# Talking-heads attention and two MLPs on one core: the first score tile issued by hand, loads in order of need, and the first two weight chunks decoded in v's buffers

## The chip, the core and the metric

One NeuronCore of a Trainium2 chip runs the whole program. Its engines are TensorE (PE in the profile; PEld is its weight load), VectorE (DVE), ScalarE (ACT), GpSimd (POOL) and SyncE (SP), which issues nearly all DMAs here; 16 DMA engines do the copies. Each engine takes its instructions in program order and waits on semaphores. The metric is the device time of one execution in microseconds, lower is better.

## What is computed

Three stages in a row, float32 in and out (the products are made of split halves, so that each needs three matmuls):

```python
scores = scale * q @ k^T                       # 4 batches, 12 heads, 448 x 448, head size 64
scores = einsum('bhij,hg->bgij', scores, w_pre)   # heads are mixed before the softmax
attn = softmax(scores)
attn = einsum('bhij,hg->bgij', attn, w_post)      # and after it
x = (attn @ v) as 1792 tokens x 768
x = ((x @ w1) * (x @ w2)) @ w3 @ w_out            # first MLP, 1024 wide
out = relu(x @ w_in)**2 @ w_out2                  # second MLP, 2048 wide
```

The MLP weights arrive as 64-bit floats and are decoded on the chip, chunk by chunk: two ACT and four DVE passes over 128 x 768 words per chunk, then a scale over two chunks, then two casts each.

## The kernel before

**Attention.** The rows of a batch are cut into four score tiles of 110, 110, 110 and 118 rows (`SUP`, s = 0 to 15). A tile is made by six calls of `qk` (two heads each: the q and k halves, three pairs of matmuls), whose results are copied from PSUM into the tile S (`evict_s` on ACT). A tile is then cut into blocks of 10 rows x 12 heads (180 blocks, `BLK`, u = 0 to 179). `regroup` is a DMA on SP's queue that puts a block's rows and heads on 120 partitions (`Bt`, five buffers, so block u+5 is issued when block u is done). The steps of a block are `premix` (PE), `negmax` (DVE), `expo` (ACT), `norm` for two blocks (DVE), `split_h` and, for odd blocks, `split_l` (POOL; for even ones DVE), `postmix` (PE), `at_h` (ACT), `at_l` (DVE), and `av` (PE) for a whole tile.

**What sets the order.** In the loop over u every engine's order is written out: a table of slots (`events`, filled by `at`) says at which u the loads, `qk`, `split_q`, `split_v` and so on are issued. What is ahead of the loop is ordered by the scheduler instead: the loads, the six `qk` of tile 0, the six of tile 1 (three ahead of the loop, three in slots 0, 2 and 4), the five first regroupings and the set-up of the mixing weights (`setup_mixers`). There DVE casts all halves of k and copies two thirds of the first tile out of PSUM, and POOL makes some of the low halves.

**The end of the attention.** From u = 164 (`mlp_start`) the buffers of q and k are given to the weights (pool `w`: two `raw` buffers, three `xa`, one `zt`). Chunks 0 (w1) and 1 (w2) are loaded on ACT's queue at u = 164 and 166, and decoded from u = 167 by `early = pair_steps(0, None)`, three steps a block. When a chunk has been decoded, `read_raw` issues the next load on SP's queue, into the same `raw` buffer. The attention result goes to DRAM (`store_x`) and comes back as x high halves (ACT's queue, `X_HIGH`, u = 165, 167, 169, 174) and low halves (SP's queue, u = 176). At u = 180 to 183 `first_tile` runs the first matmuls of the MLP between the last blocks.

**The MLPs** follow with their weights decoded in the background; no line of theirs is touched.

Of the kernel before, what the change touches and what calls it, by code (L numbers as in the profile page):

```python
# [35 lines left out]
def talking_heads_attention_moe_moe2(  # L36
# [181 lines left out]
    def qk(s, p, where=None):  # L218

# [15 lines left out]
        if where is None:  # L235
            Ps[s, p] = t
        else:
            for e in range(2):
                nc.vector.tensor_copy(Stile[s][:R, 2 * p + e, :], pt[e][:R, :S])
# [4 lines left out]


# [193 lines left out]
    def split_v(b, hg, i):  # L439
        t = vraw[b, hg]  # L440
        up = Vsc[b]
        if i == 0:
            Vt[b, hg] = tuple(
                bp.tile([CP, 6, NCH, D], F16, tag=f"V{x}", name=f"V{x}", bufs=3) for x in "hl"
            )
# [142 lines left out]
    load_k(0, 0)
    load_k(0, 1)
    load_q(0, 1)  # L590
    for p in (2, 3):
# [1 line left out]
    spare = bp.tile([P, NCH, H, RMAX], F16, tag="ATl", name="ATl")
    kraw[0, 2] = (
        spare.rearrange("p c h r -> p (c h r)").bitcast(F32)[:, : 2 * S]
        .rearrange("p (a s) -> p a s", a=2)
    )
    for p in (4, 5):
        nc.sync.dma_start(kraw[0, 2][:, p % 2, :], k[0, :, p, :])
# [922 lines left out]
```

## Time and profile before

| | us |
|---|---|
| median of 3 runs | 1301.48 (1300.58 to 1302.89) |
| the profiled execution | 1300.27 |
| its span | 1298.6 |
| PE busy in it | 1264.7 (97%) |
| DVE busy | 982.5 (76%) |
| ACT busy | 696.7 (54%) |
| POOL busy | 442.7 (34%), most of it in the attention |

The profile is one execution. Its timeline lists instructions by their start; a row with "x2" merges neighbours of one kind, and the bracket says how long the engine sat idle before it and what released it. The windows view gives each engine's busy time in a stretch. PEclk there is the granted clock of TensorE as a share of 2.4 GHz; in the first 29 us it reads 1.00 while the matmuls go at half the later pace, so for that stretch the durations are read and not this column.

### The profile page before, as it was taken

Reading aid. Unit: us, or ns where it says so; the run is one execution under the profiler, and the core shown is the slowest. Engines: PE = TensorE matmul, PEld = TensorE weight load, DVE = VectorE, ACT = ScalarE, POOL = GpSimd, SP = SyncE. Lnnn points to the kernel's source line nnn. Section 1 sums busy time; section 2 is a strip of 40 time slices with the busy share of each in tenths; the row PEclk is TensorE's granted clock in tenths of the full one; section 3 lists DMA queues with packets and bytes.
Section 4 is the critical chain, followed back from the end, with each engine's and each line's share of the span. In section 5 each row is a group of like instructions: output and inputs, shape, how many; then the busy total and the mean of one; then the engine's idle time right before and its main releaser. Section 6 shows DMA issues by size and latency. Waiting matters only on the chain. (4 is left out here: it accounts for less than half of the span.)

```text
span 1298.6 us, 25896 instructions
## 1 busy us (share of the span) xinstructions
PE 1264.7 (97%) x10173; PEld 778.9 (60%) x10173; DVE 982.5 (76%) x2036; ACT 696.7 (54%) x1349; POOL 442.7 (34%) x511
## 2 busy tenths in 40 slices
PE   7999999999999899999999999999999999999998
PEld 3676766667666555555559945555555555555555
DVE  5888898788888848887749777336669788797776
ACT  3877876877886534554324354236853453534420
POOL 3899789879877701100002200000000100001000
PEclk9999999999999999999999999999999999999999
DMA  6466555645546723424414323103131322224004
GB/s 169 114 158 163 135 143 125 166 122 157 154 119 186 208 79 82 126 79 115 138 39 155 114 75 60 31 3 86 37 78 47 102 58 60 78 37 108 11 9 170
DMA packets 82174, 132.92 MB, mean 102 GB/s; under 512 B 30820, under 2 KB 67812, under 8 KB 82052
## 3 DMA queue, kind: packets, MB, share of 16 engines
q1 hardware_dynamic: 75636, 121.87, 34.8%
q0 software_dynamic: 2992, 5.42, 2.9%
q10 hardware_dynamic: 3424, 3.98, 1.1%
q8 instruction: 80, 1.31, 0.5%
q14 instruction: 42, 0.34, 0.1%
HBM read 80.78 MB, written 11.92 MB: 71 GB/s over the span
## 5 line engine op out<-in xcount | busy, mean ns | idle before, releaser
L964 PE MATMUL mm<-x,w 128*128 128x448 f16 x2196 | 416.7, 353 | 0.9 <-DVE th L999 0.9
L964 PEld LDWEIGHTS <-w 128*128 128x128 f16 x2304 | 225.0, 98 | 210.4 <-issue 1.1
L1399 PE MATMUL mm<-w,g 128*128 128x384 f16 x1344 | 219.7, 326 | 0.0
L1399 PEld LDWEIGHTS <-g 128*128 128x128 f16 x1344 | 131.5, 98 | 87.5 <-issue 0.2
L272 PE MATMUL p<-Bt,wpre_k 120*120 120x448 f32 x360 | 163.3, 573 | 8.7 <-DMA Bt<-S 4.9
L338 POOL TENSOR_SCALAR EH<-E,st 120x448 f16<-120x448 f32 x180 | 134.9, 759 | 63.9 <-DVE st L324 46.4
L365 PEld LDWEIGHTS <-EH 120*112 120x112 f16 (+1 forms) x1440 | 125.3, 130 | 50.4 <-issue 40.3
L387 DVE TENSOR_TENSOR ATl<-o,ATh 112x480 f16<-112x480 f32 x180 | 116.1, 645 | 38.3 <-ACT ATh L381 38.2
L381 ACT CAST ATh<-o 112x480 f16<-112x480 f32 x180 | 100.8, 561 | 64.5 <-PE o L365 57.2
L365 PE MATMUL o<-wph,EH 120*112 120x120 f16 x720 | 124.9, 219 | 6.3 <-DVE ATl L387 4.7
L294 ACT ACTIVATE E<-p,st 120x448 f32<-120x448 f32 x180 | 115.7, 643 | 23.9 <-DVE st L286 10.7
L729 POOL DMA_DIRECT2D across<-tot x23 | 12.8, 555 | 324.1 <-ACT xa L715 324.1
L1408 DVE SCALAR_TENSOR_TENSOR acc<-mm,sv,acc 128x384 f32<-128x384 f32 x196 | 112.2, 610 | 14.2 <-PE mm L1399 13.5
L365 PE MATMUL o<-wpl,EH 120*112 120x120 f16 x720 | 122.7, 216 | 0.0
L365 PE MATMUL o<-wph,EL 120*112 120x120 f16 x720 | 122.7, 216 | 0.0
L286 DVE TENSOR_REDUCE st<-p 120x1 f32<-120x448 f32 x180 | 110.2, 612 | 9.4 <-PE p L272 9.2
L964 PE MATMUL mm<-h,M 128*128 128x448 f16 x576 | 109.8, 353 | 0.7 <-ACT M L1129 0.5
L350 POOL TENSOR_TENSOR EL<-F,EH 120x448 f16<-120x448 f32 (+1 forms) x90 | 101.6, 1129 | 7.5
L243 ACT COPY S<-s 110x896 f32<-110x896 f32 (+1 forms) x92 | 83.8, 911 | 29.2 <-PE s L232 28.5
L715 ACT ACTIVATE xa<-xa 128x768 f32<-128x768 f32 x56 | 47.1, 842 | 93.7 <-DVE xa L711 75.7
L352 DVE SCALAR_TENSOR_TENSOR EL<-E,st,EH 120x448 f16<-120x448 f32 (+1 forms) x90 | 84.1, 934 | 13.7 <-POOL EH L338 13.2
L365 PEld LDWEIGHTS <-EL 120*112 120x112 f16 x720 | 93.9, 130 | 0.0
(194 smaller groups left out, 2030.8 us busy)
## 6 DMA issues: line engine op xcount, KB each, us to landing
Bt<-S SPq DMA_DIRECT2D x176, 210.0 KB
raw<-in_moe_w_out_dram SPq DMA_DIRECT2D x24, 768.0 KB
raw<-in_moe_w_in_dram SPq DMA_DIRECT2D x16, 768.0 KB
raw<-in_moe_w_dram SPq DMA_DIRECT2D x14, 768.0 KB
raw<-in_moe_w_dram SPq DMA_DIRECT2D x16, 512.0 KB
vraw<-in_v_dram SPq DMA_DIRECT2D x24, 224.0 KB
out_dram<-acc SPq DMA_DIRECT2D x28, 192.0 KB
kraw<-in_k_dram SPq DMA_DIRECT2D x22, 224.0 KB
```

Source lines behind the costliest of these rows:

```text
L272: nc.tensor.matmul(pt[: n * H, :S], wpre_k.rearrange("p t g -> p (t g)")[: n * H, : n * H], Bt.pop(u)[: n * H], start=True, stop=True,)
L286: nc.vector.tensor_reduce(nsum[u][:n, 0, j : j + 1], Pp[u][:n, :S], axis=AX.X, op=ALU.max, negate=True)
L294: nc.scalar.activation(e[:n], Pp.pop(u)[:n, :S].rearrange("p (a b) -> p a b", a=EG), AF.Exp, bias=t[:n, 0, j : j + 1], scale=1.0, accum_ou ...
L338: nc.gpsimd.tensor_scalar(seven(EH[u][:n]), Ex[u][:n], inverse(u), 1.0, op0=ALU.mult, op1=ALU.mult)
L350: nc.gpsimd.tensor_tensor(a, f, b, op=ALU.subtract)
L352: nc.vector.scalar_tensor_tensor(a, e, inverse(u), b, op0=ALU.mult, op1=ALU.subtract)
L365: nc.tensor.matmul(pt[:CP, c * n : (c + 1) * n], a[:n, c * CP : (c + 1) * CP], w[:n, :n], start=(i == 0), stop=(i == 2),)
L381: nc.scalar.copy(ATs[s][0][:, :, :, m * NR : m * NR + nr], src)
L387: nc.vector.tensor_tensor(ATs[s][1][:, :, :, a], src, ATs[s][0][:, :, :, a], op=ALU.subtract)
L964: nc.tensor.matmul(pt[:, :S], w[a][:, cs], x[z][:, sl], start=(c == 0 and i == 0), stop=(c == len(parts) - 1 and i == 2),)
L1399: nc.tensor.matmul(pt[:, :OH], gs[j][a][:, ts_], ws[j][0][:, w, os_], start=(n == 0), stop=(n == 5),)
L1408: nc.vector.scalar_tensor_tensor(d, pt[:, :OH], sv[:, v : v + 1], d, op0=ALU.mult, op1=ALU.add)
```

## The change

- **Start.** The order ahead of the loop is written by hand. Loads go out as q, k0, k1, k2, the second half of q, k3 to k5, then tile 1's q, then the mixing weights, then the first three loads of v; v's other three are moved behind regroupings, at u = 1 to 3.
- For tile 0, ACT casts the high halves of four k pairs and copies most PSUM results, DVE makes all low halves of k, and POOL makes only low halves of q. All six `qk` of tile 1 and its copies stand ahead of block 0; in the loop the slots of tile 1 are gone.
- `keep_busy(n)` issues n matmuls of 128 x 512 zeros into a PSUM bank that nobody reads: 8 at the very start, 3 ahead of the first `premix`, and 2 at each of u = 1 to 4.
- **End.** Chunks 0 and 1 are loaded on SP's queue at u = 153 and 156 into the two buffers of `vraw`, whose last v is read by u = 154. Their decode works in a buffer of V's halves (`v_half`) and one of k's (`zt`), one or two steps a block: chunk 0 at u = 157 to 162, chunk 1 at u = 165 to 170, the scale and the casts at u = 171 to 178. The scale's small PSUM tiles are taken from another pool.
- Chunks 2 and 3 then find both `raw` buffers empty: they are loaded at u = 175, ahead of the loads of x's low halves. x's high halves are loaded at u = 167, 170, 173 and 176.

```diff
+    zeros = flat[:, 4 * S : 4 * S + 512]
+    nc.vector.memset(zeros, 0.0)
+    def keep_busy(n):
+        for _ in range(n):
+            nc.tensor.matmul(idle, zeros[:, :P], zeros, start=True, stop=True)
...
+    for hg in range(2):
+        load_q(1, hg)
     load_mixers()
+    for i in range(3):
+        load_v(0, 0, i)
...
+    setup_mask()
+    keep_busy(8)
+    split_q(0, 0, V)
+    for p in range(3):
+        split_k(0, p, V, A)
+        qk(0, p, WHERE[p])
+    split_q(0, 1, nc.gpsimd)
+    evict_s(0, 0)
...
+    for u in range(LEAD):
+        regroup(u)
+    split_q(1, 1, None)
+    split_ql(1, 1)
+    setup_premix()
     for p in range(NDC):
+        qk(1, p, WHERE[p])
...
+        if p == 2:
+            setup_mixers()
+    keep_busy(3)
+    FILL = {1: 2, 2: 2, 3: 2, 4: 2}
+    premix(0)
+    premix(1)
...
-        dma = nc.scalar if i < 2 else nc.sync
+            if i < 2:
+                t = v_raw().rearrange("p a d -> p (a d)").bitcast(I32)
+            else:
+                t = pools["w"].tile([P, 2 * DM], I32, tag="raw", name="raw", bufs=LOADS)
...
+                if i == 0:
+                    x = v_half("hl"[k]).rearrange("p h c d -> p (h c d)").bitcast(F32)
...
-    limit = [len(chunks)]
+    limit = [2]
...
-    X_HIGH = (1, 3, 5, 10)
+    X_HIGH = (3, 6, 9, 12)
+    v_last = first[NSUP - 4]
+    W_LOADS = (v_last + 18, v_last + 21)
+    c0, c1 = v_last + 22, first[NSUP - 1] - 3
...
+        if u == NB - LEAD:
+            limit[0] = len(chunks)
+            load_to(2 + LOADS)
-        if u - mlp_start in (0, 2):
-            load_to((u - mlp_start) // 2 + 1)
-        if u == mlp_start + 3:
-            early = pair_steps(0, None)
+        if u in W_LOADS:
+            load_to(W_LOADS.index(u) + 1)
+        if u == c0:
+            early = (x for x in pair_steps(0, None) if x[2])
```

DVE at the start of the program, before: casts (kh, qh), low halves (kl, ql) and copies into S alternate.

```order
L208 CAST qh<-qraw 128x330
L210 TENSOR_TENSOR ql<-qraw,qh 128x330
L183 CAST kh<-kraw 128x448
L185 TENSOR_TENSOR kl<-kraw,kh 128x448
L183 CAST kh<-kraw 128x448
L208 CAST qh<-qraw 128x330
L185 TENSOR_TENSOR kl<-kraw,kh 128x448
L183 CAST kh<-kraw 128x448 x2
L239 COPY S<-p 110x448 x2
L183 CAST kh<-ATl 128x448 x2
```

DVE at the same place, after (ATl is the spare buffer that holds k4, k5 and the zeros).

```order
L609 MEMSET ATl 128x256
L219 CAST qh<-qraw 128x330
L221 TENSOR_TENSOR ql<-qraw,qh 128x330
L193 TENSOR_TENSOR kl<-kraw,kh 128x448 x3
L219 CAST qh<-qraw 128x330
L193 TENSOR_TENSOR kl<-kraw,kh 128x448
L191 CAST kh<-ATl 128x448
L193 TENSOR_TENSOR kl<-ATl,kh 128x448
L191 CAST kh<-ATl 128x448
L193 TENSOR_TENSOR kl<-ATl,kh 128x448
```

ACT at the start, after; before, it had only copies of 110 x 896 ahead of the first exponential.

```order
L189 CAST kh<-kraw 128x448
L189 CAST kh<-kraw 128x448
L189 CAST kh<-kraw 128x448
L249 COPY S<-s 110x896
L189 CAST kh<-kraw 128x448
L255 COPY S<-p 110x448 x2
L255 COPY S<-o 110x448 x2
L249 COPY S<-s 110x896
L255 COPY S<-p 110x448
L217 CAST qh<-qraw 128x330
L255 COPY S<-o 110x448
```

Four of DVE's six casts of k and six of its eight copies of tile 0 have gone to ACT, and the two low halves of k that POOL made have gone to DVE.

SP's queue at the end of the attention, before: two loads of weights (raw) stand between the last regroupings.

```order
L266 DMA Bt<-S 120x1x448 x3
L655 DMA raw<-in_moe_w_dram 128x1536
L266 DMA Bt<-S 120x1x448
L512 DMA x_d<-xt 128x3x110 x2
L266 DMA Bt<-S 120x1x448 x2
L655 DMA raw<-in_moe_w_dram 128x1536
L266 DMA Bt<-S 120x1x448
L266 DMA Bt<-S 96x1x448
L519 DMA x<-x_d 128x6x448 x3
L519 DMA x<-x_d 128x6x220
```

SP's queue there, after, from the second early load (chunk 1 into vraw) to the loads of x.

```order
L721 DMA vraw<-in_moe_w_dram 128x1536
L529 DMA x_d<-xt 128x3x110 x2
L279 DMA Bt<-S 120x1x448 x6
L529 DMA x_d<-xt 128x3x110 x2
L279 DMA Bt<-S 120x1x448 x5
L529 DMA x_d<-xt 128x3x110 x2
L279 DMA Bt<-S 120x1x448 x4
L529 DMA x_d<-xt 128x3x110 x2
L279 DMA Bt<-S 120x1x448 x3
L279 DMA Bt<-S 96x1x448
L721 DMA raw<-in_moe_w_dram 128x1536 x2
L536 DMA x<-x_d 128x6x448 x3
```

No weight load stands between the last 18 regroupings any more; two now stand between the last of them and x.

## Rows read from the trace of the kernel before

**Rows 1.** Timeline of PE where the MLP begins: start, us, engine, line, instruction, idle before.

```profile
480.77 19.46 PE L964 MATMUL mm<-x,w 128*128 128x448 f16 x102 [0.86 <-DVE th L999]
```

**Rows 2.** Windows (stretch, length, busy per engine, clock, DMA), and POOL's waits.

```profile
30.60:60.00 29.40, 27.09 (x235) 17.74 (x235) 25.48 (x58) 25.29 (x61) 26.45 (x31) 1.00 0.50 130
60.00:100.00 40.00, 40.00 (x522) 27.89 (x520) 36.17 (x77) 31.89 (x70) 39.01 (x43) 1.00 0.55 145
...
POOL EH L338 <- DVE st L324: 16.4, 2, 14.1
```

**Rows 3.** Timeline of the start, all engines.

```profile
3.94 0.39 DVE L183 CAST kh<-kraw 128x448 fp32r<-128x448 f32 x1
...
5.54 0.39 DVE L183 CAST kh<-kraw 128x448 fp32r<-128x448 f32 x1 [0.56 <-DMA kraw<-in_k_dram]
...
11.34 0.58 PE L232 MATMUL o<-kh,ql 64*110 64x448 f32 x2
...
11.71 0.58 PE L232 MATMUL s<-kl,qh 64*110 64x448 f32 x2
...
17.14 7.23 SPq L266 DMA_DIRECT2D Bt<-S  x6
17.14 0.91 ACT L243 COPY S<-s 110x896 f32<-110x896 f32 x1 [3.53 <-PE s L232]
...
21.33 1.85 PE L272 MATMUL p<-Bt,wpre_k 120*120 120x448 f32 x2 [1.78 <-DMA Bt<-S]
...
29.55 0.62 DVE L286 TENSOR_REDUCE st<-p 120x1 f32<-120x448 f32 x1 [2.54 <-PE p L272]
...
30.63 1.25 POOL L338 TENSOR_SCALAR EH<-E,st 120x448 f16<-120x448 f32 x2 [14.09 <-DVE st L324]
...
31.24 1.76 PE L272 MATMUL p<-Bt,wpre_k 120*120 120x448 f32 x4
```

**Rows 4.** Windows of the start.

```profile
0.00:14.50 14.50, 7.88 (x31) 4.17 (x31) 8.43 (x19) 3.09 (x3) 6.21 (x13) 1.00 0.82 205
...
21.30:29.00 7.70, 7.67 (x18) 3.24 (x19) 1.25 (x2) 2.85 (x5) 0.00 (x0) 1.00 0.59 156
```

**Rows 5.** Windows of the end of the attention.

```profile
388.00:401.00 13.00, 13.00 (x170) 9.18 (x172) 11.21 (x25) 9.64 (x23) 11.92 (x16) 1.00 0.45 113
401.00:417.00 16.00, 14.73 (x204) 10.20 (x199) 13.02 (x27) 10.46 (x25) 10.75 (x13) 1.00 0.77 212
417.00:434.00 17.00, 12.48 (x133) 7.82 (x132) 14.74 (x28) 9.69 (x24) 11.91 (x12) 0.90 0.85 239
434.00:451.00 17.00, 15.33 (x324) 12.56 (x322) 15.31 (x40) 11.25 (x25) 13.61 (x14) 1.00 0.80 235
```

**Rows 6.** Timeline there: two waits of PE, SP's weight load, the clock's dip.

```profile
425.54 3.39 PE L272 MATMUL p<-Bt,wpre_k 120*120 120x448 f32 x4 [2.08 <-ACT E L294]
...
433.33 0.35 SPq L655 DMA_DIRECT2D raw<-in_moe_w_dram  x1
433.38 0.98 PE L272 MATMUL p<-Bt,wpre_k 120*120 120x448 f32 x2 [2.18 <-DMA Bt<-S]
...
426.00:429.00 3.00, 2.97 (x7) 0.97 (x6) 2.96 (x6) 1.37 (x4) 2.92 (x3) 0.50 1.01 290
```

**Rows 7.** Timeline there: a chunk's decode on DVE, and POOL beside it.

```profile
416.38 0.55 DVE L704 TENSOR_SCALAR xa<-raw 128x768 int32<-128x768 int32 x1
...
417.93 2.18 POOL L338 TENSOR_SCALAR EH<-E,st 120x448 f16<-120x448 f32 x2 [2.48 <-PE o L365]
...
419.64 1.27 DVE L711 SCALAR_TENSOR_TENSOR xa<-zt,xa 128x768 int32<-128x768 int32 x1
...
423.07 0.96 DVE L717 SCALAR_TENSOR_TENSOR xa<-raw,xa 128x768 int32<-128x768 int32 x1 [0.45 <-ACT xa L715]
```

**Rows 8.** Timeline there: the low halves of x, and the first MLP matmuls.

```profile
441.36 3.98 SPq L519 DMA_DIRECT2D x<-x_d  x4
...
451.04 3.58 PE L964 MATMUL p<-x,w 128*128 128x448 f16 x18
```

More of the change, by code (lines that the diff above doesn't have):

```diff
@@ L127, in load_mixers, with setup_mask @@
         )
-    def setup_mixers():
-        mask = bp.tile([NBK, NR], F32, name="mask", bufs=1)
+    mask = bp.tile([NBK, NR], F32, name="mask", bufs=1)
+    def setup_mask():
         nc.gpsimd.memset(ones, 1.0)
@@ L144, in setup_mixers @@
         )
+    def setup_mixers():
         wmax = bp.tile([P, 1], F32, name="wmax", bufs=1)
@@ L182, in split_k @@
         kT[b, p] = (hh, ll)
-        nc.vector.tensor_copy(hh, t)
+        if high is nc.scalar:
+            nc.scalar.copy(hh, t)
+        else:
+            nc.vector.tensor_copy(hh, t)
         if eng is not None:
@@ L198, in load_q, with split_q @@
         )
-    def split_q(s, hg, eng):
+    def split_q(s, hg, eng, high=None):
         R = SUP[s][2]
@@ L207, in split_q @@
         a = slice(3 * hg * R, 3 * (hg + 1) * R)
-        nc.vector.tensor_copy(hh[:, a], qraw[s][:, a])
+        if high is nc.scalar:
+            nc.scalar.copy(hh[:, a], qraw[s][:, a])
+        else:
+            nc.vector.tensor_copy(hh[:, a], qraw[s][:, a])
         if eng is not None:
@@ L234, in qk @@
                 )
[L235 to L239, printed above, removed]
+        Ps[s, p] = t if where is None else pt
     def evict_s(s, p):
@@ L442, in split_v @@
         if i == 0:
[L443 to L445 removed]
+            Vt[b, hg] = tuple(v_half(x)[:CP] for x in "hl")
         hf, lf = (x.rearrange("p h c d -> p (h c) d") for x in Vt[b, hg])
@@ L532, in at @@
         events.setdefault(slot, []).append((kind, len(events), f, a))
-    for s in range(1, NSUP):
+    for s in range(2, NSUP):
         b = SUP[s][0]
@@ L587, in talking_heads_attention_moe_moe2 @@
     load_q(0, 0)
[L588 to L591, printed above, removed]
+    for p in range(NDC):
         load_k(0, p)
[L593 to L599, printed above, removed]
-    load_mixers()
-    split_q(0, 0, nc.vector)
+        if p == 2:
+            load_q(0, 1)
@@ new lines, in talking_heads_attention_moe_moe2 @@
+    evict_s(0, 0)
+    for p in (1, 2):
+        if p == 1:
+            split_k(0, 3, V, A)
+        for e in range(2):
+            evict_one(0, p, e, A)
+    for p in range(3, NDC):
+        if p > 3:
+            split_k(0, p, V)
+        qk(0, p, WHERE[p])
+    evict_s(0, 3)
+    evict_one(0, 4, 0, A)
+    evict_one(0, 4, 1, V)
+    split_q(1, 0, None, A)
+    split_ql(1, 0)
+    evict_one(0, 5, 0, A)
+    evict_one(0, 5, 1, V)
+    for u in range(LEAD):
+        regroup(u)
+    split_q(1, 1, None)
@@ L1014, in first_tile @@
         hidden_tile(ws, sc0, hm0, i, z, begun_tiles[i], psum(ps_p, "p"))
-    for u in range(LEAD):
-        regroup(u)
-    for slot in sorted(x for x in events if x < 0):
-        for kind, _, f, a in sorted(events.pop(slot), key=lambda e: e[0]):
-            f(*a)
-    setup_mixers()
-    premix(0)
-    premix(1)
     mlp_start = first[NSUP - 1] - 4
     early = iter(())
-    order = ExitStack()
-    order.enter_context(tc.manual_schedule())
     for u in range(NB + LAG + 2):
+        if u == NB - LEAD:
+            limit[0] = len(chunks)
+            load_to(2 + LOADS)
         if u == mlp_start:
@@ L1073, in talking_heads_attention_moe_moe2 @@
         do(LOW)
-        for eng, cost, f in islice(early, 3):
-            if f:
-                f()
+        for eng, cost, f in islice(early, STEPS.get(u, 0)):
+            f()
         do(END)
         if NB <= u < NB + LAG:
-            for eng, cost, f in early:
-                if f:
-                    f()
+            assert next(early, None) is None
             allow[0] = place["w1", 2]
```

84 lines of the change are left out of this document (60 added, 24 removed).

## The prediction

> **What bounds the kernel now.** I read the end first. From 480.77 us on PE works in unbroken stretches [rows 1]; nothing of the MLPs is changed, so whatever the attention gives or takes ahead of that point should shift the end one to one. Then the windows of the attention. From 30.6 to 60 us POOL is busy 26.45 of 29.4 us, from 60 to 100 us 39.01 of 40, where PE is full too; POOL's first block step comes at 30.63 us, after a wait of 14.1 us, and in the next 90 us it waits only 16.4 - 14.1 = 2.3 us more [rows 2, 3]. So the early attention runs at POOL's pace from its first instruction, and **a start that lets POOL begin x us earlier is worth x us**. At the other end PE, full from 388 to 401 us, is busy only 14.73 of 16, 12.48 of 17 and 15.33 of 17 us up to 451 [rows 5]: 7.5 us of idle time, and three more at half clock. These two places are what the change touches.
>
> **The start: when tile 0 is whole.** Before, the first regrouping is issued at 17.14 us, when DVE has made the last copy into S [rows 3]. PE is not the bound there: a pair of matmuls of `qk` starts 0.37 us after the last (11.34 to 11.71), so a `qk` of three pairs is 1.1 us and six are 6.7. It is DVE's queue of casts, low halves and copies. After the change ACT has, up to its last copy of tile 0, four casts (on ACT not in the trace; DVE's takes 0.39, ACT's double copy 0.91 [rows 3], so 0.39 to 0.91, I take 0.5, near half the double copy), two double copies of 0.91, six half copies (taken at 0.5 too) and one cast of q (0.4, by 330 columns against 448): 2.0 + 1.8 + 3.0 + 0.4 = 7.2 us. It cannot begin before k0 is there, at about 3.94, which gives 11.1 us with no wait. It has waits: k1 lands at 5.54 [rows 3], a good us after ACT would be free, and pair 5's PSUM banks are freed by copies that stand fourth in its queue. I add 2.3 us for these: **tile 0 is whole at 13.4 us** (11.1 to 17.1). DVE's list (six low halves, two casts, two copies, q) is as long and ends no later.
>
> **The start: block 0.** From the issue of the first regrouping to its `premix` it took 21.33 - 17.14 = 4.2 us [rows 3], on idle DMA engines. After the change 18 loads are queued ahead: q 5 x 169 KB, k 6 x 229, v 3 x 229, the mixing weights 85, together 2.99 MB; before, 14.5 us x 205 GB/s = 2.97 MB had moved by 14.5 us [rows 4]. The regrouping's own bytes begin over 1 us after its issue, so the queue is empty just in time: 13.4 + 4.2 = 17.6 us. PE must be free as well: tile 1's six `qk` (q's high half is ACT's cast just ahead of its last copy, so at about 12.9) and three idle matmuls now stand ahead of `premix`. At the low clock, 1.2 GHz, which the pace of the whole start shows, that is 12.9 + 6.7 + 3 x 0.43 (448 columns take 0.37) = 20.9 us; at 2.4 GHz PE is ready by 17.6.
>
> **The start: POOL.** POOL needs three `premix` and the third `negmax`, which starts 30.63 - 29.55 = 1.1 us ahead of it [rows 3]. Before, `qk` of tile 1 stood between the first `premix`, PE was busy 7.67 of 7.70 us from 21.3 to 29 [rows 4], and a `premix` took 1.85 us at the low clock; from 31.24 on two take 1.76 [rows 3]. After the change, low clock: 20.9 + 3 x 1.85 + 1.1 = 27.6 us, a gain of 3.0. High clock: the second and third regroupings follow the first by 1.4 us each (0.21 MB at 156 GB/s [rows 4]), 17.6 + 2 x 1.4 + 1.2 + 1.1 = 22.7 us, a gain of 7.9. Eight idle matmuls keep PE at work from the first us, and `qk` of tile 1 and three more follow without holes, which is the kind of stretch after which the pace doubled before. I lean to the high end: POOL starts at 24.1, **gain 6.5 us** (3.0 to 7.9; 0 if tile 0 is not earlier). The idle matmuls at u = 1 to 4 lie in PE time that POOL's pace leaves over; without that cover the eight would cost 8 x 0.22 = 1.8 us at the high clock (448 columns take 19.46 / 102 = 0.19 [rows 1]). v's second half is issued behind block 0 and is read at u = 4 to 6, some 8 us later, so nobody waits. `setup_mixers`, a dozen small DVE steps, stands ahead of the first `negmax`; in the low case PE's three `premix` cover it, in the high one it is a part of what I hold back from the 7.9.
>
> **The end: what goes.** SP's load at 433.33 us stood in the queue until the decode had freed `raw`, and the regroupings behind it were late: PE waited 2.18 us for Bt. At 425.54 it waited 2.08 us in the middle of the decode, and after that the granted clock was 0.50, 1.2 GHz, from 426 to 429 [rows 6]: 1.7 us lost of 3.4. From 401 to 417, with two weight chunks and x on the DMA engines at 77 to 85% against 45% before [rows 5], PE lacked 1.3 us. With the chunks loaded at u = 153 and 156 and no load between the regroupings, these four should go: 2.2 + 2.1 + 1.7 + 1.3 = **7.3 us**. The nearest bounds: if DVE then sets the pace, its 43.1 us of 401 to 451 less one chunk's 3.3 (0.55 twice, 1.27, 0.96 [rows 7]) at the share of 60 to 100 us, 36.17 / 40, is 44 us of 50: 6. At most PE's whole idle time and the low clock: 9.2.
>
> **The end: what is added.** Chunk 0's decode now falls into 388 to 401 us, where PE is full, DVE at 11.21 and POOL at 11.92 of 13 us [rows 5]. DVE has 1.8 us of room for 3.3. I take **1.3 us** (0 to 3.3). Two ACT steps of 0.9 fit its 3.4 us of room. Net gain at the end 6.0 us (2.5 to 9).
>
> **The sum.** 6.5 + 6.0 = 12.5 us, so the profiled execution of 1300.27 would be 1287.8, its span 1286.1; the median of the runs lies 1.2 above that execution: **1289.0 us**.
>
> POOL's two `split_h` take 1.25 us alone and 2.18 beside DVE's decode [rows 3, 7], so a decode step that falls on POOL costs it 0.9 us. The Trainium skill, GPSIMD Engine Reference, section 1 (Specifications), says that GpSimd shares its SBUF interfaces with VectorE and is held up by VectorE instructions with two SBUF inputs; the row agrees, and the rule speaks against moving chunk 0's passes into a stretch where POOL has 1.1 us of room.
>
> **Rivals.**
> A. The idle matmuls don't raise the clock by block 0. For it: the start of before, with PE busy 7.88 of 14.5 us [rows 4], never left the low pace before some 29 us. Start 3.0 instead of 6.5: 1292.5.
> B. The decode only moves. Chunk 0's four DVE passes each cost POOL 0.9 us, 3.7 in all with 1.1 of room, as the GpSimd rows say; the end then gives 7.3 - 2.6 - 1.3 = 3.4 or less, I take 2.5: 1292.5. A and B together: 1296, and with any further miss no change.
> C. x comes late. Chunks 2 and 3 (2 x 0.79 MB, 6.7 us at 235 GB/s [rows 5]) go ahead of x's low halves, which were issued at 441.36 and first used at 451.04, 9.7 us later [rows 8]. The load of x waits for the last regrouping, 4.2 us after its issue by [rows 3], in which the chunks can move; of the other 2.5 us and of the shorter end comes a wait of 0 to 5 us, taken as 3: 1292. The Trainium skill, DMA: Bandwidth & Descriptors, section Queues, rings and completion order, says that each issuing engine has one ring on the same DMA engines and that descriptors are consumed in ring order; by that rule x stands behind both chunks, and no row of before shows two such loads on one queue.
> D. Slower: the clock stays low into the loop. Tile 1's `qk` no longer fill PE between the first blocks, and if two idle matmuls a block are too little, `premix` alone costs a block 1.85 - 0.88 = 1.0 us more, of PE time that is 27.09 of 29.4 us full already [rows 2, 3]. That is some 0.9 us a block: A's 9 us are gone after 10 blocks, and 20 blocks at 1.2 GHz give 1301.5 - 9 + 18 = 1310. Against it: PE would then be full, which before led to the high clock.
> E. The rewritten order doesn't finish tile 0 earlier, because ACT becomes what DVE was: start 0, 1295.5.
>
> **How the numbers follow.** The forecast (1285 to 1291.5) has 0.58, A 0.12, B 0.08, C 0.08, E 0.04, A and B together with nothing left 0.05, D 0.05. The range runs from both gains at the top (7.9 + 9 = 16.9: 1284.6, and 1 us for the spread of runs) to A and B together: **1283.5 to 1296.0**, which leaves out D, the joint miss and the tails of the others, under 0.2. Faster by over 0.2% (2.6 us, about what a measurement of this kernel can tell from no change): 0.90; within it 0.05; slower 0.05.
>
> **What would show it.** First `premix` at 17 to 21 us and POOL's first block step at 22.5 to 27.6 instead of 30.63; two `premix` in 1.76 us at that time (A wrong) or 3.7 (A right). POOL without new waits up to 60 us. No weight load between the last regroupings, PE's idle time from 401 to 451 us down from 7.5 to about 2, and no clock of 0.50 there. `split_h` pairs over 2 us at u = 157 to 162 would be B; a wait of the first MLP matmul for x, C. The forecast is wrong if the start's gain is given back by 120 us, or if the MLP's 818 us from its first full stretch to the end change.

## The result, and where the time went

The changed kernel takes 1288.49 us (median of 4 runs, 1287.41 to 1289.77) beside 1301.03 for the kernel before: a ratio of 0.9902, interval 0.9885 to 0.9919. The forecast was 1289.0 in 1283.5 to 1296.0, and faster. The sum is right, but its two terms are not.

The MLP didn't change: its first unbroken stretch begins at 470.22 us in place of 480.77 [rows 1], and from there to the end of the span it is 1288.1 - 470.2 = 817.9 us, before 1298.6 - 480.8 = 817.8. So all of it is won ahead of that point, and one marker in the loop shows where: ACT's `exp` of a block, one row for each of the 180 blocks. Three of the blocks, first from the kernel before, then from the changed one (start, length, engine, line, instruction; ACT's timeline):

```profile
33.47 0.64 ACT L294 ACTIVATE E<-p,st 120x448 f32<-120x448 f32 x1
...
41.75 0.64 ACT L294 ACTIVATE E<-p,st 120x448 f32<-120x448 f32 x1
...
412.82 0.63 ACT L294 ACTIVATE E<-p,st 120x448 f32<-120x448 f32 x1
```

```profile
25.44 0.64 ACT L307 ACTIVATE E<-p,st 120x448 f32<-120x448 f32 x1 [0.22 <-DVE st L323]
...
38.12 0.64 ACT L307 ACTIVATE E<-p,st 120x448 f32<-120x448 f32 x1
...
409.29 0.63 ACT L307 ACTIVATE E<-p,st 120x448 f32<-120x448 f32 x1
```

These are blocks 4, 8 and 166. Block 4 is 8.0 us earlier than before, block 8 only 3.6, and block 166, at the foot of the end, still 3.5. **More than half of what the start won is given back in four blocks**, then nothing changes for 158 blocks. The first MLP matmul is 451.04 - 440.57 = 10.5 us earlier [rows 8], so the end adds 6.9. (This trace is of the longest of the four executions, hence 10.5 and not 12.5. A second trace of the same kernel, below, has 5.2 and 6.9.)

**The start.** The changed kernel's timeline, PE's `premix` (L285 here, L272 in [rows 3]) and POOL's first block step:

```profile
17.86 0.92 PE L285 MATMUL p<-Bt,wpre_k 120*120 120x448 f32 x2
...
20.99 2.02 PE L285 MATMUL p<-Bt,wpre_k 120*120 120x448 f32 x4 [1.04 <-DMA Bt<-S]
...
23.09 1.25 POOL L351 TENSOR_SCALAR EH<-E,st 120x448 f16<-120x448 f32 x2 [8.48 <-DVE st L337]
...
30.40 0.98 PE L285 MATMUL p<-Bt,wpre_k 120*120 120x448 f32 x2 [1.98 <-DMA Bt<-S]
...
33.28 2.57 PE L285 MATMUL p<-Bt,wpre_k 120*120 120x448 f32 x4
```

POOL begins 7.5 us earlier than the 30.63 of [rows 3], one us more than forecast. But then it waits anew (POOL's waits from 23 to 60 us: what it waited for, us in sum, times, longest):

```profile
POOL EH L351 <- DVE st L337: 14.2, 4, 8.5
POOL EH L351 <- PE o L378: 1.2, 1, 1.2
```

Without the first wait of 8.5 us these are 6.9 us, where the kernel before had 2.3 [rows 2]: the 4.6 us more are about what is given back. Upstream of POOL, at 30.40, PE has waited 1.98 us for the regrouped block 7. What stood in SyncE's queue ahead of it:

```profile
13.25 6.34 SPq L279 DMA_DIRECT2D Bt<-S  x5
...
19.71 0.79 SPq L279 DMA_DIRECT2D Bt<-S  x1
20.54 1.44 SPq L414 DMA_DIRECT2D vraw<-in_v_dram  x1
22.10 1.46 SPq L279 DMA_DIRECT2D Bt<-S  x1
23.60 0.49 SPq L414 DMA_DIRECT2D vraw<-in_v_dram  x1
24.20 1.31 SPq L279 DMA_DIRECT2D Bt<-S  x1
```

The two `vraw` are thirds of v's second half, 224 KB each. They take 1.44 and 0.49 us of SyncE's time in front of block 7's `Bt` at 24.20, which PE takes up 6.2 us later; in the kernel before, the first one took 4.2 [rows 3]. What the loads cost is the late issue: without them (e9 below) the same `Bt` is issued 1.7 us earlier and taken up 6.9 us later. Right behind the wait the clock falls (stretch, length, busy time of PE, PEld, DVE, ACT, POOL, granted clock, DMA share, GB/s):

```profile
23.10:28.40 5.30, 4.79 (x26) 2.11 (x24) 3.53 (x8) 4.21 (x14) 5.22 (x7) 1.00 0.74 208
28.40:31.20 2.80, 0.82 (x3) 0.41 (x3) 1.88 (x5) 1.15 (x4) 2.68 (x4) 1.00 0.68 198
31.20:35.00 3.80, 3.80 (x28) 2.94 (x27) 2.08 (x3) 2.67 (x8) 2.26 (x3) 0.55 0.56 136
```

PE is busy 0.82 of 2.80 us, and the next 3.8 us run at 0.55, that is at 1.2 GHz for nearly all of it.

**The end.** The windows that answer to [rows 5], and the first matmul of the MLP:

```profile
388.00:401.00 13.00, 13.00 (x174) 9.32 (x174) 11.90 (x26) 11.25 (x26) 12.38 (x14) 1.00 0.56 163
401.00:417.00 16.00, 15.70 (x240) 11.41 (x238) 15.21 (x31) 11.20 (x27) 14.98 (x16) 1.00 0.62 160
417.00:434.00 17.00, 15.77 (x230) 11.15 (x225) 16.41 (x38) 12.46 (x31) 14.94 (x17) 1.00 0.91 264
434.00:441.00 7.00, 5.53 (x169) 5.13 (x164) 6.96 (x18) 3.24 (x8) 5.44 (x6) 1.00 1.10 336
...
440.57 3.58 PE L1038 MATMUL p<-x,w 128*128 128x448 f16 x18
```

Of the 33 us from 401 to 434 PE is idle 1.5, before 5.8; the clock is 1.00 throughout, before 0.90 from 417 to 434; DVE, at 16.41 of 17, is the engine that is full now.

### The profile page after: what moved, and what is told of

Same layout as the page of the kernel before. It is cut to its first block, busy times and chain, and to the rows that moved or that the text cites. A ratio compares the mean times of both kernels' runs of the same rounds, so it can differ in the third digit from the quotient of the medians.

```text
span 1288.1 us, 25945 instructions
## 1 busy us (share of the span) xinstructions
PE 1261.3 (98%) x10192; PEld 776.8 (60%) x10192; DVE 980.3 (76%) x2032; ACT 700.0 (54%) x1360; POOL 439.5 (34%) x509
## 5 line engine op out<-in xcount | busy, mean ns | idle before, releaser
L285 PE MATMUL p<-Bt,wpre_k 120*120 120x448 f32 x360 | 160.2, 563 | 5.6 <-DMA Bt<-S 3.7
L351 POOL TENSOR_SCALAR EH<-E,st 120x448 f16<-120x448 f32 x180 | 137.5, 773 | 54.5 <-DVE st L337 37.9
L307 ACT ACTIVATE E<-p,st 120x448 f32<-120x448 f32 x180 | 115.5, 642 | 26.1 <-DVE st L299 12.5
L1483 DVE SCALAR_TENSOR_TENSOR acc<-mm,sv,acc 128x384 f32<-128x384 f32 x196 | 112.1, 611 | 14.1 <-PE mm L1474 13.4
L797 POOL DMA_DIRECT2D across<-tot x23 | 12.8, 556 | 320.5 <-ACT xa L783 320.5
L365 DVE SCALAR_TENSOR_TENSOR EL<-E,st,EH 120x448 f16<-120x448 f32 (+1 forms) x90 | 82.1, 912 | 12.6 <-POOL EH L351 12.0
L1038 PEld LDWEIGHTS <-M 128*128 128x128 f16 x576 | 55.9, 98 | 53.9 <-DVE M L1200 1.9
```

The lines of the kernel that those rows point to most:

```text
L285: nc.tensor.matmul(pt[: n * H, :S], wpre_k.rearrange("p t g -> p (t g)")[: n * H, : n * H], Bt.pop(u)[: n * H], start=True, stop=True,)
L307: nc.scalar.activation(e[:n], Pp.pop(u)[:n, :S].rearrange("p (a b) -> p a b", a=EG), AF.Exp, bias=t[:n, 0, j : j + 1], scale=1.0, accum_ou ...
L351: nc.gpsimd.tensor_scalar(seven(EH[u][:n]), Ex[u][:n], inverse(u), 1.0, op0=ALU.mult, op1=ALU.mult)
L365: nc.vector.scalar_tensor_tensor(a, e, inverse(u), b, op0=ALU.mult, op1=ALU.subtract)
L1038: nc.tensor.matmul(pt[:, :S], w[a][:, cs], x[z][:, sl], start=(c == 0 and i == 0), stop=(c == len(parts) - 1 and i == 2),)
L1483: nc.vector.scalar_tensor_tensor(d, pt[:, :OH], sv[:, v : v + 1], d, op0=ALU.mult, op1=ALU.add)
```

## The experiments

Times are medians, with the ratio to the kernel before on the same chip, which took 1300.2 to 1302.0 us there. For each trace the table has how much earlier than before ACT's `exp` of five blocks and the first MLP matmul are, in us. Up to block 4 is the start as it is won, from block 8 on as it is kept; the last column less that of block 166 is the end. All are against the one trace of the kernel before.

| kernel | time | 4 | 8 | 24 | 166 | 179 | first MLP |
|---|---|---|---|---|---|---|---|
| changed, first trace | 1288.49 | 8.0 | 3.6 | 3.6 | 3.5 | 10.9 | 10.5 |
| e5 changed, second trace | 1288.05 | 7.8 | 5.2 | 5.2 | 5.2 | 12.6 | 12.2 |
| e1 end only | 1294.10 | -0.5 | -0.4 | -0.4 | -0.4 | 7.1 | 6.6 |
| e2 start only | 1297.66 | 8.6 | 5.3 | 5.3 | 5.0 | 3.2 | 3.2 |
| e3 v later | 1292.05 | 7.9 | 6.0 | 3.0 | 3.4 | 10.8 | 10.3 |
| e4 no idle matmuls | 1290.26 | 7.0 | 4.1 | 4.1 | 4.1 | 11.5 | 11.0 |
| e6 v between | 1289.95 | 8.2 | 3.6 | 3.6 | 3.9 | 11.2 | 10.8 |
| e7 decode late | 1296.04 | 8.5 | 5.3 | 5.3 | 5.6 | 5.8 | 5.2 |
| e8 chunks between | 1290.35 | 8.3 | 5.4 | 5.4 | 5.6 | 11.3 | 10.8 |
| e9 without v's second half | 1286.36 | 7.6 | 6.1 | 6.1 | 6.2 | 13.6 | 13.1 |
| e10 idle matmuls in the wait | 1288.52 | 7.2 | 5.3 | 5.3 | 5.4 | 12.8 | 12.4 |
| e11 v and its sums later | 1288.71 | 8.3 | 3.3 | 2.9 | 3.0 | 10.4 | 9.9 |
| e12 v spread | 1288.14 | 8.7 | 6.3 | 6.3 | 5.3 | 12.7 | 12.3 |

The times hold one thing more. From the first MLP matmul to the end of the span it is 847.5 us before and 847.1 to 847.7 in most traces, but 849.5 in e1, 849.2 in e3, 849.0 in e4 and 849.1 in e7. These 1.5 to 2.0 us are lost 20 to 26 us into the MLP and are no part of the start or the end: in e3 and e7 the granted clock is low there (0.53 from 461 to 464 us, 0.54 from 466 to 469), in e1 and e4 PE is idle for 1.9 and 1.4 us with no releaser that the profile shows. What causes it is open.

**The two halves apart.** e1 is the kernel before with the parts of the diff that concern the end (buffers, `W_LOADS`, `STEPS`, `X_HIGH`, `limit`), e2 with the others.

```diff
 # e1, onto the kernel before
-    X_HIGH = (1, 3, 5, 10)
+    X_HIGH = (3, 6, 9, 12)
...
-        if u - mlp_start in (0, 2):
-            load_to((u - mlp_start) // 2 + 1)
-        if u == mlp_start + 3:
-            early = pair_steps(0, None)
+        if u in W_LOADS:
+            load_to(W_LOADS.index(u) + 1)
+        if u == c0:
+            early = (x for x in pair_steps(0, None) if x[2])
```

> The start of the kernel before, the end of the changed one: chunks 0 and 1 loaded at u = 153 and 156 on SyncE's queue into v's buffers and decoded from u = 157 on, chunks 2 and 3 behind the last regrouping. Theory S (read from the trace after: the start's gain of 8 us at block 4 is down to 3.6 at block 8, the end gives 7): ACT's exp of block 150 at the same time as before, within 0.3 us, first MLP matmul some 7 us earlier than 451.04, so about 1294.0 where the kernel before has 1301.0. Theory P (the sum of the prediction): the end gives 6.0, 1295.0. Rival: the end gains its 7 only because the loop comes to it earlier or in another phase; then under 4, 1297 or more.

Measured: 1294.10, ratio 0.9949 (0.9932 to 0.9965). From block 166 to the first MLP matmul it wins 6.58 + 0.35 = 6.9 us, as in the first and the second trace of the whole change (10.5 - 3.5 and 12.2 - 5.2): the end is worth 6.9 by itself, whenever the loop comes to it; so it is in all ten traces that have the whole new end. Theory S held; the sum of the prediction, 6.0, was one us short.

> The start of the changed kernel, the end of the one before. Theory S: block 4 is some 8 us earlier than before, block 8 some 3.6, and that stays to block 150; 1297.5 against 1301.0, a gain of 3.5. Theory P: 6.5 us of the start reach the end, 1294.5. If the old end gives back more (it has its own late load), under 3.

Measured: 1297.66, ratio 0.9975 (0.9965 to 0.9984), a gain of 2.8. Theory S had the time (1297.5), by another way: in its trace 8.6 us are won at block 4, 5.3 and not 3.6 kept at block 8, and 3.2 reach the MLP. The old end takes 1.8 of them in this execution, with a longer stretch at the low clock than the kernel before has (0.90 in [rows 5]):

```profile
417.00:434.00 17.00, 14.41 (x153) 10.09 (x153) 14.46 (x29) 10.43 (x25) 10.40 (x11) 0.72 0.80 227
```

So the start alone is worth 3, and 5 in front of the new end.

**Is one trace the rule?** e5 is the changed kernel again, with no edit.

> The changed kernel again, unchanged, for a second trace and beside the three that follow. The stretch to block 150 is instruction for instruction that of the run with the start alone, whose trace kept 5.3 us at block 8, where the first trace of the changed kernel kept 3.6. Theory U (the give-back varies with when the transfers land, 2 to 5 us of the 8): a gain between 3.5 and 5.5 us at block 12, the end's 7.4 us from block 166 to the first MLP matmul, 1288 to 1289. Rival (the first trace is the rule): 3.6 again.

Measured: 1288.05, ratio 0.9899 (0.9882 to 0.9916). Theory U held for the start and the time; the end is 6.9 us and not its 7.4. The Bt wait is shorter, and the clock stays (timeline of PE and a window of this run):

```profile
30.12 0.98 PE L285 MATMUL p<-Bt,wpre_k 120*120 120x448 f32 x2 [1.54 <-DMA Bt<-S]
...
31.20:35.00 3.80, 3.72 (x41) 2.50 (x40) 2.63 (x4) 2.88 (x9) 2.44 (x4) 1.00 0.57 136
```

A wait of 1.98 us and a clock of 0.55 leave 3.6 us at block 8, a wait of 1.54 with the clock at 1.00 leaves 5.2. At block 6, behind the wait, the two differ by 5.5 - 4.9 = 0.6; the other 1.0 is lost between blocks 6 and 8, where the first trace has the low clock.

**What takes the start's gain.** Four edits to v's second half. e3 moves the loads from u = 1 to 3 to u = 4 to 6, and everything that reads them three slots back.

```diff
+                d = 0 if b else 3
-                    at(f - 4 + 3 * hg + i if b else i + 1, LOAD, load_v, b, hg, i)
-                at(f + 3 * hg + i + 1, MID, sum_v, b, hg, i)
-                at(f + 3 * hg + i + 13, MID, split_v, b, hg, i)
...
+                    at(f - 4 + 3 * hg + i if b else i + 1 + d, LOAD, load_v, b, hg, i)
+                at(f + 3 * hg + i + 1 + hg * d, MID, sum_v, b, hg, i)
+                at(f + 3 * hg + i + 13 + d, MID, split_v, b, hg, i)
...
```

> The changed kernel with the three loads of v's second half at u = 4 to 6 instead of 1 to 3, and what reads them (sums, scale, splits) three slots later. Theory Q (the load of v ahead of the regroupings of blocks 6 and 7 in one queue makes TensorE wait 2 us for Bt at 28.4 to 30.4, and the low clock that follows costs 1.3 more): no wait for Bt over 0.5 us before 35 us, no granted clock of 0.5 there, the gain of 8 us at block 4 mostly kept, 1284 to 1285.5. Rival R (the wait only moves to the regroupings of blocks 9 to 11, where the loads now stand): a Bt wait of some 2 us between 32 and 42 us, 1287 to 1289. Rival T (something else, GpSimd or TensorE at its own pace, would take the gain back in any case): no Bt wait, but the gain at block 12 is down to about 3.6 all the same, 1288.5.

Measured: 1292.05, ratio 0.9934 (0.9919 to 0.9949), 3.6 us more than the changed kernel, of which 1.7 in its trace are the longer MLP. Up to block 16 it goes theory Q's way in the main: no wait for Bt over 0.74 us, where it had said 0.5, and 5.4 to 8.1 us kept. Then 3.5 of them go, for a reason that no theory had. The waits from 45 to 75 us (engine, what it waited for, us, times, longest) show, beside `premix` waiting 2.0 us for `expo`, `av` waiting for v's halves and the PSUM of the scale's two small matmuls waiting for ACT:

```profile
PEld s L443 <- ACT S L249: 1.5, 1, 1.5
PEld s L449 <- ACT S L249: 1.5, 1, 1.5
PEld L493 <- DVE Vl L472: 1.3, 1, 1.3
```

The readers had no three slots to give. e6 goes the other way: the three loads right behind the first five regroupings.

```diff
...
     for u in range(LEAD):
         regroup(u)
+    for i in range(3):
+        load_v(0, 1, i)
     split_q(1, 1, None)
```

> The changed kernel with the three loads of v's second half right behind the first five regroupings, ahead of the sixth, in place of one each behind the sixth, seventh and eighth; what reads v stays where it is. Theory Q (the order in the queue of loads of v and regroupings makes the Bt wait at block 7): wait for Bt at blocks 6 to 8 under 1 us in sum, the gain at block 12 is 6 us or more, and since v is there in time nothing is lost at blocks 13 to 24 as in the run with v later: 1285.5 to 1287. Rival R (the queue is short of bandwidth whatever the order): the wait moves ahead to blocks 4 to 6, gain at block 12 as in the changed kernel, 1288.5. Rival T (another engine's pace takes it back): no Bt wait, gain at block 24 under 4.5 us, 1288.5.

Measured: 1289.95, ratio 0.9909 (0.9893 to 0.9925). Rival R held: the wait is longer and stands two blocks earlier, with the fall of the clock behind it.

```profile
27.12 0.98 PE L285 MATMUL p<-Bt,wpre_k 120*120 120x448 f32 x2 [2.73 <-DMA Bt<-S]
...
28.40:31.20 2.80, 2.80 (x17) 1.99 (x16) 1.05 (x3) 0.68 (x2) 1.75 (x2) 0.52 0.54 146
```

e9 leaves these bytes out; heads 6 to 11 of the first batch then read the first half's v.

```diff
-                if b or hg:
+                if b:
...
+        if b == 0:
+            vraw[0, 1] = vraw[0, 0]
```

> The changed kernel without the three loads of v's second half: heads 6 to 11 of the first batch read the first half's tile, so the output is not the reference's; every step on the engines stays. 0.67 MB and three entries of SyncE's queue are gone. Theory Q2 (the give-back of 2.5 to 4.5 us comes from these bytes, in whatever place they are queued: behind the sixth regrouping the wait was at block 7, ahead of it at block 5): no Bt wait over 0.7 us, the gain of about 8 us at block 4 is at 7 or more at block 24 and stays, about 1286. That would also bear out that early attention runs at GpSimd's pace and x us earlier are worth x. Rival T (another engine's pace takes it back, the Bt wait only marks the place): 5.2 us or less at block 24, 1288.

Measured: 1286.36, ratio 0.9887 (0.9870 to 0.9903). The interval overlaps the changed kernel's, the trace tells more (SyncE's queue; PE):

```profile
22.50 1.69 SPq L279 DMA_DIRECT2D Bt<-S  x1
...
29.43 0.98 PE L285 MATMUL p<-Bt,wpre_k 120*120 120x448 f32 x2 [0.72 <-DMA Bt<-S]
```

Between the theories: 6.1 us are kept, 0.9 more than in the second trace and 2.5 more than in the first, but 1.5 of the 7.6 go without them, with a Bt wait of 0.7 at block 7. So v's bytes cost the start 0.9 to 2.5 us; half of the 1.5 is still a wait for the regrouping, and what takes the other 0.7 I haven't found.

e11 loads as late as e3 and moves only the sums and the scale's first three steps, so that nothing behind u = 12 shifts.

```diff
-                    at(f - 4 + 3 * hg + i if b else i + 1, LOAD, load_v, b, hg, i)
-                at(f + 3 * hg + i + 1, MID, sum_v, b, hg, i)
+                    at(f - 4 + 3 * hg + i if b else i + 4, LOAD, load_v, b, hg, i)
+                at(f + 3 * hg + i + (1 if b or not hg else 4), MID, sum_v, b, hg, i)
...
+        steps = ((7, MID), (9, END)) if b else ((10, MID), (10, END))
...
```

> The changed kernel with v's second half loaded at u = 4 to 6 and summed at 7 to 9, the scale's steps pushed together so that they end at u = 12 as in the changed kernel, and nothing moved behind them. Theory Q (v's bytes ahead of the regroupings of blocks 6 and 7 cost the start 2.5 us or more; in the run with v later 6 to 7 us were kept at block 12 and lost when TensorE waited for the shifted splits): gain at block 12 of 6 us or more, and it stays: 1285.5 to 1287.3, faster than both. Rival (the crowded sums and scale steps cost what the Bt wait did, or the wait only moves to blocks 9 to 11): 1288 or more.

Measured: 1288.71, ratio 0.9907 (0.9892 to 0.9922). My theory fell: 7.4 us at block 7, then the wait stands at block 9, and 2.9 are left.

```profile
33.71 1.27 PE L285 MATMUL p<-Bt,wpre_k 120*120 120x448 f32 x2 [2.08 <-DMA Bt<-S]
```

**The clock.** e4 has no idle matmul, e10 nine more of them where PE waits.

```diff
 # e4
-        for _ in range(n):
+        for _ in range(0):
             nc.tensor.matmul(idle, zeros[:, :P], zeros, start=True, stop=True)
 # e10
+                if x == 7:
+                    keep_busy(9)
                 if x < NB:
                     premix(x)
```

> The changed kernel without any idle matmul. Theory P (its rival A): the first qk runs at 0.37 us a pair step and not 0.2, first premix near 21 us instead of 17.9, GpSimd's first block step at about 27 instead of 23.1; 4 us of the start lost there. Theory S (the Bt wait behind v's loads sets blocks 6 to 8): what is lost at the start is mostly not lost at block 8, since the give-back shrinks; gain at block 8 between 2 and 3.6, 1288.5 to 1290.5. Rival: all of the loss reaches the end, 1292 to 1293; or the low clock stays into the loop, over 1293.

Measured: 1290.26, ratio 0.9918 (0.9904 to 0.9933): by the interval not told apart from the changed kernel, and 1.5 us of its trace are the longer MLP. Theory P fell, with the first `premix` at 18.59 and not near 21. The clock rises without any idle matmul (PE's timeline; the pace is the distance of two starts):

```profile
4.53 0.71 PE L242 MATMUL s<-kh,qh 64*110 64x448 f32 x2 [4.53 <-ACT kh L189]
...
12.38 0.58 PE L242 MATMUL o<-kh,qh 64*110 64x448 f32 x2
12.76 0.58 PE L242 MATMUL o<-kl,qh 64*110 64x448 f32 x2
...
13.87 0.36 PE L242 MATMUL s<-kl,qh 64*110 64x448 f32 x2
...
15.04 0.37 PE L242 MATMUL p<-kl,qh 64*110 64x448 f32 x2
15.25 0.37 PE L242 MATMUL p<-kh,ql 64*110 64x448 f32 x2
...
18.59 0.61 PE L285 MATMUL p<-Bt,wpre_k 120*120 120x448 f32 x1 [0.27 <-DMA Bt<-S]
```

From 4.5 us on two starts are 0.37 to 0.8 us apart, from 10.9 to 13 some 0.38 without a hole (1.2 GHz), from 13.9 on 0.2 (2.4 GHz). The kernel before kept the low pace to 29 us, though PE was busy 7.67 of the last 7.70 [rows 4], so a stretch without holes alone doesn't tell when the clock rises. With the idle matmuls, in the first trace of the changed kernel, the high pace is there by 7.5 us:

```profile
7.50 0.37 PE L242 MATMUL p<-kh,ql 64*110 64x448 f32 x2
7.70 0.36 PE L242 MATMUL o<-kh,qh 64*110 64x448 f32 x2
```

It needn't stay: in e5 it falls once more (window of that run), behind waits of at most 0.63 us.

```profile
10.00:13.00 3.00, 3.00 (x18) 1.96 (x16) 2.21 (x5) 2.18 (x5) 0.41 (x1) 0.50 0.75 222
```

The idle matmuls bring `premix` 0.7 us, of which nothing can be seen at block 8.

> The changed kernel with nine idle matmuls (1.9 us) between premix of block 6 and of block 7, where TensorE waits for Bt. Theory C (the wait of 2 us lets the clock fall and that costs 1.3 to 1.5 us more in the executions where it is that long; 3.5 us kept in the first trace against 5.2 in the second): no granted clock under 1 from 28 to 36 us, gain at block 12 5 to 5.7 us, 1287.5 to 1288.5. Rival (the clock falls for another reason, or the idle matmuls get in the way of the postmix behind them): gain under 4.5 us, 1289 or more.

Measured: 1288.52, ratio 0.9905 (0.9890 to 0.9920). Theory C held as far as it went: the clock stays at 1.00 from 23 to 40 us and 5.3 us are kept, no more than e5 keeps by itself. It says something else by accident: in this execution the clock was at 0.50 from 14.3 to 17.7 us and the start was late, block 1 by 1.5 us against e5, and block 8 is as early as there. Its regrouping was issued at 27.31 us, in e5 at 27.37. **What decides is when the regrouped blocks land, not when POOL begins.**

**The end.** e7 loads the two chunks as early as the changed kernel but runs all twenty decode steps from u = 167 on, three a slot, as before (the scratch `zt` of chunk 0 then comes from pool `w` again). e8 puts chunks 2 and 3 back between the last regroupings, with their buffers free.

```diff
 # e7
-                    if k == 0:
+                    if k == 2:
...
-    STEPS.update({c1 + 6 + i: 1 for i in range(8)})
+    STEPS = {c1 + 2 + i: 3 for i in range(7)}
 # e8
+        if u in (c1 + 5, c1 + 8):
+            limit[0] += 1
+            load_to(limit[0])
         if u == NB - LEAD:
```

> The changed kernel with the chunks loaded as early as in it, but all twenty decode steps of the pair from u = 167 on, three a slot, as in the kernel before. Theory V (the decode's steps crowded on VectorE between blocks 167 and 175 cost the 2.1 us wait, the 1.7 of low clock behind it and some of 1.3): the end loses 3.5 to 5 of its 7.4 us, 1292 to 1293.5. Rival W (what the end gains is the queue: no chunk and no x between the last regroupings): it loses 1 us or less, 1289 to 1289.5.

Measured: 1296.04, ratio 0.9955 (0.9939 to 0.9972). Rival W fell, and V was too small: the whole end is gone (5.2 - 5.6 = -0.3 us where the others have 6.9). The trace shows why: one wait for DVE, and then the clock (PE's timeline; windows).

```profile
417.40 0.21 PE L378 MATMUL o<-wph,EH 120*112 120x120 f16 x1 [1.85 <-DVE ATl L400]
...
425.54 0.58 PE L845 MATMUL s<-wm,ones 2*128 2x2 f32 x2 [2.31 <-DVE wm L840]
...
414.00:417.00 3.00, 1.55 (x37) 1.41 (x36) 2.31 (x4) 1.89 (x6) 2.92 (x4) 1.00 0.48 138
417.00:420.00 3.00, 2.02 (x15) 0.90 (x14) 2.97 (x8) 2.26 (x5) 1.12 (x2) 0.75 0.77 219
420.00:423.00 3.00, 3.00 (x15) 1.88 (x15) 2.00 (x3) 1.39 (x3) 2.92 (x4) 0.50 0.45 114
423.00:426.00 3.00, 0.69 (x4) 0.46 (x2) 2.96 (x8) 1.18 (x3) 0.99 (x1) 0.50 0.60 143
426.00:429.00 3.00, 3.00 (x16) 2.14 (x17) 2.86 (x10) 1.74 (x4) 2.44 (x4) 0.50 0.15 31
429.00:432.00 3.00, 3.00 (x23) 1.93 (x23) 1.84 (x4) 1.99 (x5) 0.93 (x1) 0.50 0.90 257
432.00:435.00 3.00, 3.00 (x63) 2.40 (x58) 2.96 (x7) 1.91 (x5) 1.26 (x3) 0.98 0.99 260
```

After a wait of 1.85 us the granted clock is at 0.50 to 432 us, and a second wait falls in that stretch: some 13 us at 1.2 GHz, where the kernel before had three [rows 6]. No load stands between the last regroupings here, and no wait for Bt is left; what the early decode buys is a PE that doesn't wait for DVE. Another 1.6 us of this trace are the longer MLP. The Trainium skill, TensorE: Matmul & The Clock Gate, section HAM oscillation, describes such a kernel: a wait lets the clock fall, and the work behind it starts at half rate. The trace agrees, with 0.50 behind 1.85 us; the section's waits are longer and for transfers, here it was VectorE.

> The changed kernel with the loads of chunks 2 and 3 at u = 170 and 173, between the last regroupings, where the kernel before has them, instead of behind the last one. Their buffers are free here, so SyncE's queue waits for nothing; only the bytes are in the way. Theory X (before, the loss of 2.2 us was the wait for the buffer at the queue's head, not the bytes): under 0.7 us lost, 1288.5 to 1289.2. Rival Y (0.79 MB at 235 GB/s ahead of a regrouping are 3.4 us, and TensorE waits for Bt behind each): 2 to 4 us lost, 1290.5 to 1292.5.

Measured: 1290.35, ratio 0.9913 (0.9895 to 0.9930); the interval overlaps the changed kernel's, but the trace counts it: the end wins 10.8 - 5.6 = 5.2 in place of 6.9, and PE waits three times for Bt, 2.3 us in sum, where e5's trace has none.

```profile
422.62 0.98 PE L285 MATMUL p<-Bt,wpre_k 120*120 120x448 f32 x2 [1.32 <-DMA Bt<-S]
...
430.97 0.98 PE L285 MATMUL p<-Bt,wpre_k 120*120 120x448 f32 x2 [0.59 <-DMA Bt<-S]
...
432.38 0.96 PE L285 MATMUL p<-Bt,wpre_k 96*96 96x448 f32 x2 [0.43 <-DMA Bt<-S]
```

Theory X fell: the bytes alone are worth 1.7 us, nearly the 2.2 that the prediction gave to the wait at the queue's head. The first of the three waits is at block 175, where the kernel before waits 2.18 [rows 6]. Y's 3.4 for each load was too much; I take it that most of a load passes while PE is busy with earlier blocks, which no run shows apart.

**A better version?** e12 puts the first third of v's second half ahead of all regroupings and the others at u = 2 and 4, and keeps e10's idle matmuls.

```diff
-                if b or hg:
-                    at(f - 4 + 3 * hg + i if b else i + 1, LOAD, load_v, b, hg, i)
+                if b or hg and i:
+                    at(f - 4 + 3 * hg + i if b else 2 * i, LOAD, load_v, b, hg, i)
...
+    load_v(0, 1, 0)
```

> The changed kernel with the first third of v's second half ahead of the first regrouping, the second at u = 2 and the last at u = 4 (summed one slot later), and nine idle matmuls ahead of premix of block 7. Without those bytes 6.1 us of the start were kept, with them 3.5 to 5.3. Theory Z (a later first premix costs nothing, since the run with the idle matmuls began 1.4 us later at block 1 and had the same 5.3 us at block 8; what costs is a load of v in front of a regrouping that is needed within some 5 us): first premix about 1 us later, wait for Bt at blocks 6 to 9 under 1 us, gain at block 12 of 5.5 to 6.1, 1287 to 1288, at best 1 us better than the changed kernel, which the timing can hardly tell. Rival R (the bytes cost what they cost, wherever they stand): gain at block 12 of 5.3 or less, 1288.3 or more.

Measured: 1288.14, ratio 0.9909 (0.9894 to 0.9924). Its trace has 6.3 us at block 8, as much as e9 keeps without the bytes, but it doesn't test theory Z: the first `premix` is at 18.07 us, only 0.2 later than in the changed kernel, block 4 is earlier than there, and the idle matmuls fill the time in which a wait for Bt would show. At block 36 another wait for Bt, 0.8 us, takes 1.1 of that, and the time is the changed kernel's. Nothing that I ran beats it by what can be measured.

## Why the prediction was right, point by point

**The MLP follows one to one**: right for the changed kernel, 817.9 us against 817.8, and in most of the other traces; e1, e3, e4 and e7 lose 1.5 to 2.0 us in it.

**Tile 0, first `premix`, POOL's start**: right. Forecast 13.4, 17.6 and 24.1 us, measured 13.25 (the issue of the first regrouping), 17.86 and 23.09; two `premix` take 2.02 us, not 3.7, so A didn't come, nor E. The reason given for the clock holds by half: behind the idle matmuls the pace is high by 7.5 us, but they weren't needed, since e4 has none and is at the high pace from 13.9 us on, ahead of `premix`. That the clock stood high when `premix` came was luck in part: in e10, with the same idle matmuls, it was low from 14.3 to 17.7 and `premix` began at 19.62.

**"A start that lets POOL begin x us earlier is worth x us"**: this step failed. POOL began 7.5 us earlier and kept 3.6 to 5.2 of them; up to 60 us it waits 6.9 us where it had 2.3, so my sign "POOL without new waits up to 60 us" didn't come. I read POOL's few waits between 30 and 60 us as a bound, but they describe a start in which the regroupings had a lead: in the kernel before, SyncE's queue was done with block 5's regrouping while PE still worked through tile 1 at half clock. As I read it, with that cover gone the blocks come faster than SyncE's queue can feed them: five regroupings take 6.34 us of it, and one is taken up 4 to 7 us after its issue. The trace of e10, late by 1.5 us at block 1 and level at block 8, shows it, and e9, which gives back 1.5 us without v's bytes.

**"v's second half is issued behind block 0 and is read 8 us later, so nobody waits"**: the second step that failed. I looked for the readers of v and not for who stands behind the loads in the queue: the regroupings of blocks 6 to 8. The Trainium skill, DMA: Bandwidth & Descriptors, section Queues, rings and completion order, says that one issuing engine's descriptors are consumed in ring order on each DMA engine; the wait that moved with the loads, from block 7 to block 5 in e6 and to block 9 in e11, agrees. Whether SyncE's own time or the rings hold the regroupings up, no run tells apart. Together the two steps make 6.5 into 5.2, and 3.5 where the wait is long enough for the clock to fall. The start was forecast too high, though within its own range of 3.0 to 7.9.

**The end, what goes**: 7.3 us forecast, 6.9 measured in sum, and the cost of chunk 0's decode in the full stretch was 0 and not 1.3: in e5's trace the lead is 5.2 us at block 150 and 5.2 at block 166. B's sign did appear there: POOL's pairs of `split_h` take 2.47 us at 391.44 and 2.18 at 396.12, where the kernel before has 1.25 in each. The Trainium skill, GPSIMD Engine Reference, section Specifications, names VectorE instructions with two SBUF inputs, or in a 2-port mode, as those that contend with GpSimd. The trace agrees for the second pair, beside which DVE runs a pass with two (0.95 us at 396.85); beside the first stand decode passes with one, and their mode no row here shows. It costs the end nothing, and PE is the engine that is full there (13.00 of 13).

**Its four parts** were not four losses to be added. By e7 nothing of the 6.9 is left without the early decode, by e8 the place of the last loads is worth 1.7. A wait in this stretch can cost itself and the low clock behind it, as in e7, so whichever is left can spend what the others saved; that this is why the four don't add is argued and not tested. One reading was off, too: the weight load ahead of the late block 175 was the first one, issued at 424.09 us with that block's `Bt` at 424.54 behind it. The load at 433.33 [rows 6] came after, and PE didn't wait for the two regroupings behind it. PE's idle time from 401 us to the first MLP matmul is 3.0 us, where I had said about 2.

**C**: no wait of the first MLP matmul for x in either trace. **D**: wrong the other way; in the loop the clock fell for under 4 us in the first trace and not at all in e5, never for 20 blocks.

So the forecast of 12.5 us stands on 6.5 + 6.0, and the runs show 5.2 + 6.9: two errors of opposite sign, of about one us each (of three and one in the first trace). That they cancel is luck, and the total is no proof of the terms.

## What to carry to other kernels

Before a gain at one engine's first instruction is counted in full, ask what supply had been running ahead under cover of the time that goes, and follow a marker block by block until the lead is steady: here it took 8 blocks of 180 to know what the start was worth. Of a transfer that is moved, look at whoever stands behind it in its queue, not only at its reader. And where TensorE is nearly full, a wait of two us is not two us: spread other engines' work so that PE never stops, before shortening anything.

## What the hardware showed that I had not expected

- The clock rises without idle matmuls: `qk` runs from 4.5 us on and is at 2.4 GHz from about 13.5 (e4). The column of the granted clock reads 1.00 there all the time, also in the stretch of [rows 4] whose pace is half; only the distance of two starts tells it.
- It falls after less than I thought, and not by the length of one wait: it fell behind 1.85 us (e7) and 1.98 (first trace), and in e5 at 9.7 us behind waits of 0.2 to 0.63, while 1.54 us in e5 and 1.79 in e4 left it up. And it can stay low for long: some 13 us in e7, with PE busy for most of them.
- SyncE itself is full at the start: issuing a regrouping or a load of v takes it 0.5 to 1.8 us, and from 13.25 to 28.2 us of the first trace no hole between two of them is over 0.12 us.
- Executions of one kernel go with it too. Of nine of the kernel before, beside e5, the shortest is 1299.61 us at a mean granted clock of 0.999, the longest 1304.30 at 0.991.
